# Attention and two feed-forward layers: weight conversions inside the attention steps, at other steps and on other engines

## The chip, the cores and the metric

The kernel runs on one core of one Trainium2 chip. The metric is the device time of one execution in microseconds (us), here the median of several runs. A profile is one execution, taken apart by engine: PE (TensorE), DVE (VectorE), ACT (ScalarE), POOL (GpSimd) and SP (SyncE, which here issues the transfers).

## The reference

Attention over 2 batches, 8 heads, 768 tokens and head size 64, with a bias that falls with distance and a mask (8 global keys and a window of 96), then two feed-forward layers of 512 to 2048 to 512, over 1536 tokens:

```
scores = q @ k^T / sqrt(D) - slope_h * dist        (masked where neither global nor local)
a = exp(scores - max)
a = a / (sum(a) + 1e-9)
x = a @ v
h = x @ w_in;   x = (h * tanh(softplus(h))) @ w_out
h = x @ w_in2;  x = bent(h) @ w_out2               (0 below -1, h above 1, a parabola between)
```

The weights arrive as 64-bit floats. The kernel turns each into a sum of two rounded 32-bit parts (hi and lo) on the chip, and each product of the layers is three matmuls: hi by hi, lo by hi and hi by lo.

## The kernel before

The attention runs in 24 steps, three for each of the 8 pairs of heads (2 batches by 4); a step is two blocks of 128 queries for the two heads of a pair. `attention_windows` writes the steps in a software pipeline, and the order that is written is the order on every engine (the schedule is manual). In step s stand, in this order: SyncE's loads; the rounding of finished outputs (`x_hi`, ScalarE); the scores of step s+1, the transposes of step s-2 and the value products of step s-3 (TensorE); the first half of the scores of step s (`softmax`: a reduction on VectorE that adds the bias, then the exponential on ScalarE, which also sums the totals); `normalise` of step s-1; the lower parts of the outputs (`x_lo`, VectorE); the eviction of one half of the transposes (ScalarE); the second half of the scores; the eviction of the other half (VectorE); and then what the table `BESIDE` (L36) names for step s.

`normalise` (L347) takes the totals of a step: it adds 1e-9 (VectorE, L349), forms the reciprocal (VectorE, L350) and scales the probabilities with it (four operations on GpSimd, L354). The transposes of that step read what is scaled. `st` is the small tile of the totals, `pr` the probabilities, `pts` the evicted transposes.

The table's entries are pieces of other work. `b2` to `b7` are the bias of one head (384 columns by a slope), on the engine that `BIAS_ON` names. The other names stand for one operation on one half (512 columns) of one of the first three weight blocks. The digit behind the letter is the block, the last one the half:

- T: `top` (L223), scales the upper words in place in the landing area (GpSimd, by `FIRST_ON`)
- B: `low` (L227), part of the lower words into `wbits` (ScalarE)
- V: `signed_value` (L246): the sign bits into `wbits` (VectorE, L233), and then shift and join (VectorE, L236)
- H: `high` (L240), the rounding of `wbits` to the hi part `whi` (ScalarE)
- R: `rest` (L243), what remains, to the lo part `wlo` (VectorE)

So T00 is the scaling of the first half of block 0. `wbits` holds one block at a time. A block is one transfer of 1 MB; blocks 0 and 1 land in the two `stage` buffers, block 2 in `third`. These loads stand in SyncE's queue between those of queries, keys and values (`wts.load` in L396; two more follow where V11 and V21 stand).

From step 23 on the entries h0a, h0b, h1a, h1b and g0a to g0c are the first pieces of the feed-forward layers, which then run on TensorE to the end. The functions that the diff touches, and what calls them:

Of the kernel before, what the change touches and what calls it, by code (L numbers as in the profile page):

```python
# [13 lines left out]
U16 = mybir.dt.uint16  # L14
I64 = mybir.dt.int64
AF = mybir.ActivationFunctionType
ALU = mybir.AluOpType
# [10 lines left out]
PRE = 3  # L28

BIAS_ON = "vvappppv"  # L30
FIRST_ON = "ppaavv"
LATER_ON = "aaaavv"

BESIDE = {  # L36
# [5 lines left out]
}  # L42


@with_exitstack
def attention_then_two_ffn_kernel(
# [10 lines left out]
    nc = tc.nc  # L57
    B, NP, _, S = q.shape
    H, D = 2 * NP, P // 2
# [49 lines left out]
    first = ctx.enter_context(tc.tile_pool(name="first", bufs=1))  # L109
# [31 lines left out]
    words = raw.bitcast(U32).rearrange("p (n two) -> p n two", two=2)  # L141
# [46 lines left out]
    class Weights:  # L188
# [15 lines left out]
        def convert(self, pool, m, f):  # L204


            hi, lo = (pool.tile([P, 2, DM], F32R, tag=f"w{n}{f}", name=f"w{n}{m}_{f}") for n in ("hi", "lo"))
            self.parts[m, f] = (hi, lo)
            first = m == 0 and f < PRE
            out = wbits  # L210

            def words(dtype, i, k):
                n = 8 // mybir.dt.size(dtype)
                return self.landing(m, f).bitcast(dtype).rearrange("p (a n w) -> p a n w", a=2, w=n)[:, i, :, k]

            bits = out.rearrange("p a (n two) -> p a n two", two=2)
            on = FIRST_ON if first else LATER_ON

            def moved(i, dtype):

                return words(dtype, i, 1) if first else wsc[:, i].bitcast(dtype)

            def top(i):  # L223

                scaled(on[i], moved(i, F32), words(F32, i, 1), 2.0 ** -112)

            def low(i):  # L227

                nc.scalar.activation(bits[:, i, :, 0], words(U16, i, 1), AF.Copy, scale=2.0 ** -13,  # L229
                                     bias=2.0 ** -14 - 0.5)  # L230

            def sign(i):
                nc.vector.tensor_scalar(bits[:, i, :, 1], words(U16, i, 3), 0x8000, None, op0=ALU.bitwise_and)  # L233

            def value(i):
                nc.vector.scalar_tensor_tensor(out[:, i].bitcast(U32), moved(i, U32), 3,  # L236
                                               out[:, i].bitcast(U32),
                                               op0=ALU.logical_shift_left, op1=ALU.bitwise_or)

            def high(i):  # L240
                rounded(on[2 + i], hi[:, i], out[:, i].bitcast(F32))

            def rest(i):  # L243
                remainder(on[4 + i], lo[:, i], out[:, i].bitcast(F32), hi[:, i])

            def signed_value(i):  # L246
                sign(i)
                value(i)

            def begin():  # L250

                if self.late:
                    self.late.pop(0)()
                top(0)
                low(0)
                sign(0)

            def middle():
                if self.late:
                    self.late.pop(0)()  # L260
                value(0)

            def end():
                top(1)
                low(1)
                sign(1)
                self.load()
                high(0)
                value(1)
                rest(0)  # L270
                self.late = [lambda: high(1), lambda: rest(1)]

            named = {f"{c}{f}{i}": lambda part=part, i=i: part(i) for i in range(2)
                     for c, part in (("T", top), ("B", low), ("V", signed_value), ("H", high), ("R", rest))}
            return named, (begin, middle, end)

        def finish(self):
# [8 lines left out]
    def attention_windows(x_hi, x_lo, bank, wts, opening):  # L286
        with ExitStack() as es:
# [58 lines left out]

            def normalise(s):  # L347
                pr, st = probs[s]
                nc.vector.tensor_scalar(st[..., 2], st[..., 1], 1e-9, None, op0=ALU.add)  # L349
                nc.vector.reciprocal(st[..., 3], st[..., 2])  # L350
                for u in range(2):
                    n = keys(2 * steps[s][2] + u)
                    for j in range(2):
                        nc.gpsimd.tensor_scalar(pr[:, u, j, 0:n], pr[:, u, j, 0:n], st[:, u, j, 3:4], 1.0,  # L354
                                                op0=ALU.mult, op1=ALU.mult)
# [37 lines left out]
                bias_of(h)  # L393
            for s in range(-1, NU + 4):

                if s in (0, 4, 10):  # L396
                    wts.load()
                if s >= 2 and s % 3 == 2 and s // 3 + 3 < len(pairs):
                    load_qk(rp, *pairs[s // 3 + 3])
                if s >= 6 and s % 3 == 0 and s // 3 + 1 < len(pairs):  # L400
                    vs[pairs[s // 3 + 1]] = load_v(rp, *pairs[s // 3 + 1])
                ready, done[:] = done[:], []
                for hi, lo, src in ready:
                    rounded("a", hi, src)
                if s + 1 < NU:
                    scores(s + 1)
                if 0 <= s - 2 < NU:
                    transposes(s - 2)
                if 0 <= s - 3 < NU:
                    values(s - 3)  # L410
                if 0 <= s < NU:
                    softmax(s, 0)
                if 0 <= s - 1 < NU:
                    normalise(s - 1)
                for hi, lo, src in ready:
                    remainder("v", lo, src, hi)
                if 0 <= s - 2 < NU:
                    evict(s - 2, 0)
                if 0 <= s < NU:
                    softmax(s, 1)  # L420
                if 0 <= s - 2 < NU:
                    evict(s - 2, 1)
                for name in BESIDE.get(s, ()):
                    opening[name]()
                    if name in ("V11", "V21"):
                        wts.load()


    def attention_all(x_hi, x_lo, bank, wts, opening):
        with ExitStack() as es:  # L430
# [31 lines left out]
            for b in range(B):  # L462
                for p in range(NP):
# [6 lines left out]
                    for j in range(2):  # L470
                        h = 2 * p + j
                        ro = slice(j * D, (j + 1) * D)
                        for pv, (t0, n) in zip(pvs, pieces):
                            for i in range(t0 // P, (t0 + n) // P):
# [3 lines left out]
                                for u, (k0, kn) in enumerate(((0, 4), (4, NB - 4))):  # L478
                                    for c in range(kn):
# [3 lines left out]
                                                            scale, None, op0=ALU.mult)  # L483
# [20 lines left out]
                                                     pT[:, c], start=(c == 0), stop=(c == NB - 1))  # L504
                    for pv, (t0, n) in zip(pvs, pieces):
                        split(x_hi[b][:, p, t0:t0 + n], x_lo[b][:, p, t0:t0 + n], pv)
            for name in sum((BESIDE[s] for s in sorted(BESIDE)), ()):
                if name[0] != "b":
                    opening[name]()
                    if name in ("V11", "V21"):  # L510
                        wts.load()
# [256 lines left out]
```

## Time and profile before

| | us |
|---|---|
| median of 3 runs | 626.03 (625.89 to 627.49) |
| span of the profiled execution, first to last instruction | 624.8 |
| PE busy in it | 603.2 |
| DVE busy | 419.2 |
| ACT busy | 390.8 |
| POOL busy | 53.2 |

The record gives the profiled execution no time other than its span; the median of the runs lies 1.2 us above that. Busy time counts instructions, not waits. Matmuls are pipelined, so TensorE's busy time is not a measure of how near to its peak it works. GpSimd works in the first 86 us alone, and all that the change touches lies there.

### The profile page before, as it was taken

Reading aid. Unit: us, or ns where it says so; the run is one execution under the profiler, and the core shown is the slowest. Engines: PE = TensorE matmul, PEld = TensorE weight load, DVE = VectorE, ACT = ScalarE, POOL = GpSimd, SP = SyncE. Lnnn points to the kernel's source line nnn. Section 1 sums busy time; section 2 is a strip of 40 time slices with the busy share of each in tenths; the row PEclk is TensorE's granted clock in tenths of the full one; section 3 lists DMA queues with packets and bytes.
Section 4 is the critical chain, followed back from the end, with each engine's and each line's share of the span. In section 5 each row is a group of like instructions: output and inputs, shape, how many; then the busy total and the mean of one; then the engine's idle time right before and its main releaser. Section 6 shows DMA issues by size and latency. Waiting matters only on the chain.

```text
span 624.8 us, 9737 instructions
## 1 busy us (share of the span) xinstructions
PE 603.2 (97%) x3584; PEld 510.7 (82%) x3584; DVE 419.2 (67%) x979; ACT 390.8 (63%) x848; POOL 53.2 (9%) x116
## 2 busy tenths in 40 slices
PE   5899899999999999999999999999999999999995
PEld 4677678888888888888888888888888888888884
DVE  6799969999999777797887876564333333433332
ACT  5899968888888566686776777574433333433332
POOL 3675630000000000000000000000000000000000
PEclk9988999999999999999999999999999999999999
DMA  7996302443333202121321422300100000100002
GB/s 201 310 287 229 116 1 69 135 135 121 102 122 131 68 1 68 68 83 59 129 69 67 135 69 73 129 1 1 67 1 1 1 1 0 68 0 2 0 1 72
DMA packets 10422, 49.85 MB, mean 80 GB/s; under 512 B 1408, under 2 KB 1664, under 8 KB 6272
## 3 DMA queue, kind: packets, MB, share of 16 engines
q1 hardware_dynamic: 10224, 48.90, 24.3%
q8 instruction: 30, 0.49, 0.3%
q10 hardware_dynamic: 144, 0.26, 0.1%
q14 instruction: 24, 0.20, 0.1%
HBM read 46.01 MB, written 3.15 MB: 79 GB/s over the span
## 4 chain that ended last, share of the span: by engine, by line
PE 88%; DVE 5%; ACT 3%; issue 1%; POOL 1%; DMA 1%; SPq 1%; POOLq 0%; DVEq 0%; ACTq 0%
PE psum L581 22%; PE psum L590 21%; PE psum L524 14%; PE psum L525 14%; PE psum L527 14%; ACT pr L344 2%; DVE pr L339 2%; PE psum L387 1%; PE psum L327 1%; POOL pr L354 1%; PE psum L368 1%; DVE pts L172 1%; DVE wbits L236 1%; DMA qr<-in_q_dram 1%; ACT pts L170 0%
## 5 line engine op out<-in xcount | busy, mean ns | idle before, releaser
L524 PE MATMUL psum<-x_hi,whi 128*128 128x512 f32 x448 | 157.1, 360 | 0.0
L525 PE MATMUL psum<-x_lo,whi 128*128 128x512 f32 x448 | 157.0, 360 | 0.0
L527 PE MATMUL psum<-x_hi,wlo 128*128 128x512 f32 x448 | 106.1, 359 | 0.0
L524 PEld LDWEIGHTS psum<-x_hi,whi 128*128 128x128 f32 x448 | 84.4, 188 | 14.8 <-issue 0.7
L525 PEld LDWEIGHTS psum<-x_lo,whi 128*128 128x128 f32 x448 | 84.5, 189 | 12.8
L527 PEld LDWEIGHTS psum<-x_hi,wlo 128*128 128x128 f32 x448 | 77.7, 189 | 12.5
L570 DVE TENSOR_TENSOR g_lo<-e,g_hi 128x512 fp32r<-128x512 f32 (+1 forms) x113 | 66.1, 608 | 31.6 <-ACT g_hi L568 31.5
L548 ACT ACTIVATE e<-psum 128x512 f32<-128x512 f32 (+1 forms) x49 | 28.8, 589 | 88.5 <-PE psum L527 88.5
L568 ACT ACTIVATE g_hi<-e 128x512 fp32r<-128x512 f32 (+1 forms) x113 | 59.8, 557 | 34.8 <-DVE e L553 31.2
L549 DVE TENSOR_SCALAR e<-e 128x512 f32<-128x512 f32 (+1 forms) x49 | 20.7, 422 | 83.8 <-ACT e L548 83.7
L590 PE MATMUL psum<-whi,g_hi 128*128 128x512 f32 x192 | 74.8, 390 | 0.0
L590 PE MATMUL psum<-whi,g_lo 128*128 128x512 f32 x192 | 74.7, 389 | 0.0
L590 PE MATMUL psum<-wlo,g_hi 128*128 128x512 f32 x192 | 74.7, 389 | 0.0
L581 PE MATMUL psum<-g_lo,whi 128*128 128x512 f32 (+1 forms) x256 | 67.2, 343 | 0.0
L581 PE MATMUL psum<-g_hi,wlo 128*128 128x512 f32 (+1 forms) x256 | 65.8, 338 | 0.0
L581 PE MATMUL psum<-g_hi,whi 128*128 128x512 f32 (+1 forms) x256 | 65.7, 338 | 0.0
L533 ACT ACTIVATE e<-psum 128x512 f32<-128x512 f32 x64 | 31.2, 492 | 51.3 <-PE psum L527 50.8
L553 DVE TENSOR_TENSOR e<-psum,e 128x512 f32<-128x512 f32 (+1 forms) x49 | 33.4, 681 | 30.7 <-ACT e L550 30.5
L344 ACT ACTIVATE pr<-pr,st 128x256 f32<-128x256 f32 (+1 forms) x96 | 46.0, 481 | 8.8 <-DVE st L339 7.7
L229 ACT ACTIVATE wbits<-stage 128x512 uint16<-128x512 uint16 x62 | 48.4, 781 | 1.3 <-DMA stage<-in_w_dram 1.3
L236 DVE SCALAR_TENSOR_TENSOR wbits<-wsc,wbits 128x512 uint32<-128x512 uint32 x58 | 40.2, 693 | 12.7 <-ACT wbits L229 9.5
L354 POOL TENSOR_SCALAR pr<-pr,st 128x256 f32<-128x256 f32 (+1 forms) x96 | 45.3, 492 | 28.0 <-ACT pr L344 12.6
(66 smaller groups left out, 896.2 us busy)
## 6 DMA issues: line engine op xcount, KB each, us to landing
stage<-in_w_dram SPq DMA_DIRECT2D x31, 1024.0 KB, 4.9
vr<-in_v_dram SPq DMA_DIRECT2D x8, 704.0 KB, 9.4
kr<-in_k_dram SPq DMA_DIRECT2D x14, 216.0 KB, 10.4
out_dram<-stage SPq DMA_DIRECT2D x11, 256.0 KB, 2.3
qr<-in_q_dram SPq DMA_DIRECT2D x7, 384.0 KB, 10.5
third<-in_w_dram SPq DMA_DIRECT2D x1, 1024.0 KB, 12.2
kr<-in_k_dram SPq DMA_DIRECT2D x2, 144.0 KB, 3.4
qr<-in_q_dram SPq DMA_DIRECT2D x1, 256.0 KB, 3.5
```

The source lines that it names most:

```text
L229: nc.scalar.activation(bits[:, i, :, 0], words(U16, i, 1), AF.Copy, scale=2.0 ** -13, bias=2.0 ** -14 - 0.5)
L236: nc.vector.scalar_tensor_tensor(out[:, i].bitcast(U32), moved(i, U32), 3, out[:, i].bitcast(U32), op0=ALU.logical_shift_left, op1=ALU.bit ...
L344: nc.scalar.activation(pr[:, u, j, 0:n], pr[:, u, j, 0:n], AF.Exp, scale=-1.0, bias=st[:, u, j, 0:1], accum_out=st[:, u, j, 1:2])
L354: nc.gpsimd.tensor_scalar(pr[:, u, j, 0:n], pr[:, u, j, 0:n], st[:, u, j, 3:4], 1.0, op0=ALU.mult, op1=ALU.mult)
L524: nc.tensor.matmul(ph, wh[:, c], xh[:, c, tok], start=(c == 0), stop=False)
L525: nc.tensor.matmul(ph, wh[:, c], xl[:, c, tok], start=False, stop=False)
L527: nc.tensor.matmul(ph, wl[:, c], xh[:, c, tok], start=False, stop=(c == KD - 1))
L553: nc.vector.tensor_tensor(e, ph, e, op=ALU.max)
L568: nc.scalar.activation(hi[:, t0:t0 + n], e, AF.Copy)
L570: nc.vector.tensor_tensor(lo[:, t0:t0 + n], e, hi[:, t0:t0 + n].bitcast(F32), op=ALU.subtract)
L581: nc.tensor.matmul(y, lhs[:, w], rhs[:, t0:t0 + n], start=(f == 0 and i == 0 and c % share == 0), stop=(f == NF - 1 and i == 2 and c % sha ...
L590: nc.tensor.matmul(ys[c], lhs[:, w], rhs, start=(f == 0 and i == 0), stop=(f == NF - 1 and i == 2))
```

## The change

The table of what stands beside the attention becomes two tables. `BESIDE` keeps what stands at the end of a step. `AHEAD` names one GpSimd operation a step, put inside `normalise`, behind the reciprocal in the code and ahead of the four scalings. V is split: S (the sign) becomes an entry of its own and V is shift and join alone. Of the first three blocks, T and now S run on GpSimd; H and R both run on VectorE (`FIRST_ON`). The addition of 1e-9 moves to GpSimd. The entries move: T00 from the end of step 5 to `normalise` in step 6, B00 from step 6 to 8, V00 from 7 to 9, H00 from 8 to 10, and so on; the last R moves from step 22 to 21. The second and third load of a block move from steps 4 and 10 to 3 and 7.

```diff
-FIRST_ON = "ppaavv"
+FIRST_ON = "ppvvvv"
...
 BESIDE = {
-    1: ("b2", "b3"), 3: ("b4",), 4: ("b5",), 5: ("T00",), 6: ("b6", "T01", "B00"), 7: ("b7", "V00", "B01"),
-    8: ("V01", "H00"), 9: ("H01", "R00"), 11: ("R01", "T10", "B10"), 12: ("T11", "V10", "B11"),
-    13: ("V11", "H10"), 14: ("R10", "H11"), 16: ("R11",), 17: ("T20", "B20"), 18: ("T21", "V20", "B21"),
-    19: ("V21", "H20"), 20: ("R20", "H21"), 22: ("R21",),
+    1: ("b2",), 6: ("b7",), 8: ("B00",), 9: ("V00",), 10: ("H00", "R00", "B01"), 11: ("V01",),
+    12: ("H01", "R01", "B10"), 13: ("V10",), 14: ("H10", "R10", "B11"), 15: ("V11",), 16: ("H11", "R11"),
+    17: ("B20",), 18: ("V20",), 19: ("H20", "R20", "B21"), 20: ("V21",), 21: ("H21", "R21"),
     23: ("h0a",), 24: ("h0b",), 25: ("g0a", "h1a", "g0b"), 26: ("g0c", "h1b"),
 }
+AHEAD = {
+    1: ("b3",), 2: ("b4",), 4: ("b5",), 5: ("b6",), 6: ("T00",), 7: ("S00",), 8: ("T01",), 9: ("S01",),
+    10: ("T10",), 11: ("S10",), 12: ("T11",), 13: ("S11",), 15: ("T20",), 16: ("S20",), 17: ("T21",), 18: ("S21",),
+}
...
             def sign(i):
-                nc.vector.tensor_scalar(bits[:, i, :, 1], words(U16, i, 3), 0x8000, None, op0=ALU.bitwise_and)
+                to, word = bits[:, i, :, 1], words(U16, i, 3)
+                if first:
+                    nc.gpsimd.tensor_scalar(to, word, 32768.0, 32768.0, op0=ALU.is_ge, op1=ALU.mult)
+                else:
+                    nc.vector.tensor_scalar(to, word, 0x8000, None, op0=ALU.bitwise_and)
...
             def normalise(s):
                 pr, st = probs[s]
-                nc.vector.tensor_scalar(st[..., 2], st[..., 1], 1e-9, None, op0=ALU.add)
+                nc.gpsimd.tensor_scalar(st[..., 2], st[..., 1], 1e-9, 1.0, op0=ALU.add, op1=ALU.mult)
                 nc.vector.reciprocal(st[..., 3], st[..., 2])
+                for name in AHEAD.get(s + 1, ()):
+                    opening[name]()
...
-                if s in (0, 4, 10):
+                if s in (0, 3, 7):
                     wts.load()
```

GpSimd's order from the scaling of step 4 to that of step 7, before. `pr4` is the probability tile of step 4, `stage0` the landing area of block 0 (the first such row is T00, the second T01), and `bias` here the entry b6:

```order
L354 TENSOR_SCALAR pr4_341<-pr4_341,st4_342 128x256 x4
L166 TENSOR_SCALAR stage0_77<-stage0_77 128x512
L354 TENSOR_SCALAR pr5_391<-pr5_391,st5_392 128x256 x4
L166 TENSOR_SCALAR bias_180<-wsc_80 128x384
L166 TENSOR_SCALAR stage0_77<-stage0_77 128x512
L354 TENSOR_SCALAR pr6_441<-pr6_441,st6_442 128x128 x2
L354 TENSOR_SCALAR pr6_441<-pr6_441,st6_442 128x256 x2
L354 TENSOR_SCALAR pr7_492<-pr7_492,st7_493 128x256 x4
```

The same stretch now (L352 is the addition to the totals, L169 with `stage0` T00 and then T01, L238 the sign S00):

```order
L169 TENSOR_SCALAR bias_180<-wsc_80 128x384
L359 TENSOR_SCALAR pr4_341<-pr4_341,st4_342 128x256 x4
L352 TENSOR_SCALAR st5_392<-st5_392 128x4
L169 TENSOR_SCALAR stage0_77<-stage0_77 128x512
L359 TENSOR_SCALAR pr5_391<-pr5_391,st5_392 128x256 x4
L352 TENSOR_SCALAR st6_442<-st6_442 128x4
L238 TENSOR_SCALAR wbits_79<-stage0_77 128x512
L359 TENSOR_SCALAR pr6_441<-pr6_441,st6_442 128x128 x2
L359 TENSOR_SCALAR pr6_441<-pr6_441,st6_442 128x256 x2
L352 TENSOR_SCALAR st7_493<-st7_493 128x4
L169 TENSOR_SCALAR stage0_77<-stage0_77 128x512
L359 TENSOR_SCALAR pr7_492<-pr7_492,st7_493 128x256 x4
```

T00 still stands between the scalings of step 4 and step 5; T01 stands one scaling later than before, b6 earlier, a sign has come in, and an addition stands ahead of each step's scalings.

VectorE's order through the end of step 12, before (L172 evicts the transposes of step 10; L233 is the sign and L236 the shift and join of V10, the first half of block 1):

```order
L172 COPY pts10_726<-psum_143 128x8x64
L233 TENSOR_SCALAR wbits_79<-stage1_78 128x512
L236 SCALAR_TENSOR_TENSOR wbits_79<-stage1_78,wbits_79 128x512
L339 ISA pr13_801,st13_802<-psum_143,bias_180 128x256
L339 ISA st13_802 128x1
L339 ISA pr13_801,st13_802<-psum_143,bias_180 128x256
L339 ISA st13_802 128x1
L349 TENSOR_SCALAR st12_750<-st12_750 128x4
L350 RECIPROCAL st12_750<-st12_750 128x4
```

And now (L175 CAST is the rounding H01, L178 the remainder R01, both of block 0; L353 is the reciprocal):

```order
L175 COPY pts10_724<-psum_143 128x8x64
L175 CAST whi0_0_146<-wbits_79 128x512
L178 TENSOR_TENSOR wlo0_0_147<-wbits_79,whi0_0_146 128x512
L342 ISA pr13_799,st13_800<-psum_143,bias_180 128x256
L342 ISA st13_800 128x1
L342 ISA pr13_799,st13_800<-psum_143,bias_180 128x256
L342 ISA st13_800 128x1
L353 RECIPROCAL st12_748<-st12_748 128x4
```

The addition has left VectorE, and a rounding and a remainder of block 0 stand where the sign and the value of block 1 stood.

## Rows read from the trace of the kernel before

**Rows 1.** Busy us (instructions) by stretch: PE, PEld, DVE, ACT, POOL; clock; DMA; GB/s

```profile
35.50:60.00 24.50, 22.47 (x298) 19.32 (x298) 23.90 (x101) 23.09 (x79) 15.64 (x32) 0.93 0.86 257
60.00:82.50 22.50, 19.20 (x261) 15.84 (x257) 22.04 (x86) 21.38 (x73) 14.88 (x31) 1.00 0.30 106
82.50:95.00 12.50, 12.50 (x121) 10.13 (x120) 7.52 (x20) 6.90 (x18) 3.13 (x7) 1.00 0.00 1
```

**Rows 2.** Waits of the attention: who waited for whom, us, times, longest

```profile
DVE st L349 <- ACT pr L344: 0.9, 2, 0.6
```

**Rows 3.** GpSimd in order of time: start, us, operation, [idle before, what ended it]

```profile
26.60 0.65 POOL L166 TENSOR_SCALAR stage<-stage 128x512 f32<-128x512 f32 x1 [4.14 <-DMA stage<-in_w_dram]
27.22 1.85 POOL L354 TENSOR_SCALAR pr<-pr,st 128x256 f32<-128x256 f32 x4
```

**Rows 4.** Block 0: its issue in time; then its size and us to landing

```profile
11.58 0.52 SPq L202 DMA_DIRECT2D stage<-in_w_dram  x1
...
stage<-in_w_dram SPq DMA_DIRECT2D x1, 1024.0 KB, 14.9
```

**Rows 5.** TensorE in order of time, first and last of six groups without a pause

```profile
27.76 1.84 PE L368 MATMUL psum<-ident,pr 64*128 64x64 f32 x16 [2.44 <-POOL pr L354]
...
35.48 1.14 PE L327 MATMUL psum<-kr,qr 64*128 64x256 f32 x8
```

**Rows 6.** VectorE's groups to 84 us: busy, mean ns; last row ns least/median/most

```profile
L349 DVE TENSOR_SCALAR st<-st 128x4 f32<-128x4 f32 x24 | 4.8, 201 | 1.3 <-ACT pr L344 0.9
L175 DVE TENSOR_TENSOR wlo<-wbits,whi 128x512 fp32r<-128x512 f32 x6 | 4.6, 773 | 0.0
...
L175 DVE TENSOR_TENSOR wlo<-wbits,whi x6: 679/725/908, 38.1 to 80.0; 128x512 fp32r<-128x512 f32 x6
```

**Rows 7.** VectorE in order of time: the sign-and-value pairs of steps 12 and 19

```profile
47.14 0.74 DVE L233 TENSOR_SCALAR wbits<-stage 128x512 uint16<-128x512 uint16 x1
...
48.85 0.41 DVE L339 CUSTOM_DVE_ANT_0 pr<-psum,bias 128x256 f32<-128x256 f32 x1
...
70.67 0.51 DVE L233 TENSOR_SCALAR wbits<-third 128x512 uint16<-128x512 uint16 x1
71.29 0.74 DVE L236 SCALAR_TENSOR_TENSOR wbits<-third,wbits 128x512 uint32<-128x512 uint32 x1
71.95 0.41 DVE L339 CUSTOM_DVE_ANT_0 pr<-psum,bias 128x256 f32<-128x256 f32 x1
```

**Rows 8.** VectorE in order of time: a clamp with one input and its successor

```profile
90.41 0.43 DVE L535 TENSOR_SCALAR e<-e 128x512 f32<-128x512 f32 x1 [0.44 <-ACT e L533]
90.87 0.69 DVE L536 SCALAR_TENSOR_TENSOR e<-e 128x512 f32<-128x512 f32 x1
```

**Rows 9.** Two remainders on VectorE and the scaling on GpSimd at the same time

```profile
54.97 0.48 POOL L354 TENSOR_SCALAR pr<-pr,st 128x256 f32<-128x256 f32 x1
...
55.08 0.91 DVE L175 TENSOR_TENSOR wlo<-wbits,whi 128x512 fp32r<-128x512 f32 x1
...
60.47 0.73 DVE L175 TENSOR_TENSOR wlo<-wbits,whi 128x512 fp32r<-128x512 f32 x1
...
60.63 0.91 POOL L354 TENSOR_SCALAR pr<-pr,st 128x256 f32<-128x256 f32 x1
```

**Rows 10.** GpSimd: T in blocks 0 and 1 (ns least/median/most); one scaling of 128x128

```profile
L166 POOL TENSOR_SCALAR stage<-stage x4: 651/770/1120, 26.6 to 47.5; 128x512 f32<-128x512 f32 x4
...
59.48 0.38 POOL L354 TENSOR_SCALAR pr<-pr,st 128x128 f32<-128x128 f32 x1 [0.73 <-PE psum L368]
```

**Rows 11.** TensorE in order of time: the first hidden block's first matmul

```profile
82.47 0.50 PE L524 MATMUL psum<-x_hi,whi 128*128 128x512 f32 x1
```

**Rows 12.** The last query load of pair 5: issue, us to landing, first scores

```profile
29.19 0.33 SPq L96 DMA_DIRECT2D qr<-in_q_dram  x1
...
qr<-in_q_dram SPq DMA_DIRECT2D x1, 384.0 KB, 13.2
...
50.28 1.05 PE L327 MATMUL psum<-kr,qr 64*128 64x128 f32 x7 [0.96 <-DVE st L339]
```

More of the change, by code (lines that the diff above doesn't have):

```diff
@@ L244, in rest @@
                 remainder(on[4 + i], lo[:, i], out[:, i].bitcast(F32), hi[:, i])
-            def signed_value(i):
-                sign(i)
-                value(i)
             def begin():
@@ L273, in convert @@
             named = {f"{c}{f}{i}": lambda part=part, i=i: part(i) for i in range(2)
-                     for c, part in (("T", top), ("B", low), ("V", signed_value), ("H", high), ("R", rest))}
+                     for c, part in (("T", top), ("S", sign), ("B", low), ("V", value), ("H", high), ("R", rest))}
             return named, (begin, middle, end)
@@ L506, in attention_all @@
                         split(x_hi[b][:, p, t0:t0 + n], x_lo[b][:, p, t0:t0 + n], pv)
-            for name in sum((BESIDE[s] for s in sorted(BESIDE)), ()):
+            for name in sum((AHEAD.get(s, ()) + BESIDE.get(s, ()) for s in range(28)), ()):
                 if name[0] != "b":
```

## The prediction

> **What bounds the kernel now.** I read four views, in this order. First the busy time by stretch [rows 1]. From 82.5 us on TensorE is busy in all of the next 12.5 us, and no later work depends on the attention steps, so whatever moves the start of that stretch moves the end of the kernel one to one. Before it, in the attention steps, VectorE is the fullest engine: 23.90 of 24.5 us, then 22.04 of 22.5 us, with ScalarE close behind at 23.09 and 21.38 and GpSimd at about two thirds. The change is therefore priced as VectorE time inside the attention steps, up to the moment when TensorE starts the first hidden block at 82.47 us [rows 11].
>
> Second, the waits [rows 2]: VectorE seldom has to wait for the exponentials' totals. Third, GpSimd's order in time [rows 3]: it sits idle for 4.14 us before T00, the first scaling of a weight block, and the scaling of step 5 stands behind T00. T00 cannot begin before its megabyte has landed: issued at 11.58 us, 14.9 us to landing, so 26.5 us [rows 4]. Fourth, TensorE behind it: the transposes for step 5 start at 27.76, one scaling after T00, and six groups of matmuls follow each other without a pause until the scores at 35.48 us, of which the first and the last are shown [rows 5].
>
> **What cannot change: everything up to 35.5 us.** The words "begun later" suggest that this wait goes. It does not. In the changed order T00 still stands between the total of step 5 and the scaling of step 5, so the scaling still follows T00 and T00 still follows the landing at 26.5 us. Nothing ahead of this load in SyncE's queue is moved. The load of the second block stands in the same place of the queue as before (its step number changes, the order does not); only the third block's load goes ahead of the keys and queries of pair 5 and the values of pair 4, which then land some 4.1 us later (1 MB at the 257 GB/s of that stretch [rows 1]). The last query piece of pair 5 was issued at 29.19 us and landed 13.2 us later, at 42.4; its first scores start at 50.28 [rows 12]. So it lands at 46.5 us, in time; without this cover of 7.9 us the 4.1 would stand on the path.
>
> So gains of the first six steps (GpSimd's extra total, bias work one per step, VectorE's freed time) end in the same wait, and TensorE's gapless chain to 35.48 starts at the same moment. What differs at 35.5 us is what has been done: the old order has V00 and V01 behind it there, the new one has both still ahead, because B00 and B01 stand at steps 8 and 10.
>
> **VectorE from step 9 to the end of attention, before.** The totals: 15 additions of 201 ns [rows 6] = 3.0 us. Sign and value pairs: four (steps 12, 13, 18, 19), from the sign's start to the next step's first instruction 1.71 us in the first and 1.28 in the last [rows 7], 5.9 us in all four. Remainders: six at 773 ns [rows 6], of which 0.08 us overlap with the next instruction (the value at 71.29 ends at 72.03, the next starts at 71.95 [rows 7]), so 0.70 each = 4.2 us. Together 13.1 us.
>
> **The same, after.** Six values, six roundings, six remainders. A remainder that meets nothing is 0.68 us, the least of the six [rows 6], 0.60 with its overlap; a value, with two inputs of the same size, I put at 0.61. A rounding (a copy of 128x512 from SBUF to SBUF on VectorE) is not in the trace. The nearest row below is the clamp at 90.41, one input and the same size, 0.43 us and 0.46 to a next instruction that needs its result [rows 8]; the nearest above is a remainder, 0.60. I take 0.46, as it has one input like the clamp. The Trainium skill ("VectorE: DVE Perf Modes", the perf-mode tier table) gives fp32 copies and one-input operations in SBUF twice the rate of a two-input operation; the clamp against the least remainder agrees, 0.43 to 0.68. Sum without collisions: 6 x (0.61 + 0.46 + 0.60) = 10.0 us, 3.1 us less than before.
>
> **Collisions take part of it back.** VectorE and GpSimd hold each other up when VectorE works on two SBUF inputs. At 55.08 a remainder takes 0.91 us, while a scaling runs until 55.45; at 60.47 one takes 0.73, and the scaling that starts within it 0.91 instead of 0.48 [rows 9]. Against 0.68 VectorE loses 0.05 to 0.23 us, 0.14 in the middle, and GpSimd about 0.43. Now 12 groups (six values; six rounding-and-remainder pairs) stand just where GpSimd is scaling: 12 x 0.14 = 1.7 us. Bounds: none, and 0.23 for each of 18 instructions, 4.1 us.
>
> **The hop of the totals.** VectorE's reciprocal now waits for an addition on GpSimd, which stands behind the scaling of the step before, and behind the reciprocal wait the x remainder, the second half of the scores and the eviction on VectorE. An addition on 128x4 is not in the trace; a scaling of 128x256 takes 0.48 us [rows 9] and one of 128x128 0.38 [rows 10], so extrapolated to no elements 0.28 us, and with the passing on some 0.35 (an estimate). It costs only where VectorE is there before the total is: before the change it had to wait for the exponentials in 2 of 24 steps, 0.9 us [rows 2]. I take 0.4 us; bounds 0 and 1.8 (a third of 15 x 0.35).
>
> **GpSimd** then does in a step an addition 0.28, a T or sign operation of about 0.65, and four scalings 1.85 [rows 3, 10]: 2.8 us, plus about 0.4 lost to VectorE, against steps of 3.1 us (15 steps from 35.48 to 82.47 [rows 5, 11]). It has next to no room left, but is not the bound. ScalarE loses six roundings, some 3 us, and is not the bound from step 9 to 21.
>
> **Sum:** 10.0 + 1.7 + 0.4 = 12.1 against 13.1 us: TensorE's dense part starts 1.0 us earlier. On the profiled execution, span 624.8 to 623.8 us. The median of the runs, 626.03, is 1.2 above the span, so 625.0 us. The measurement of this kernel tells about 0.3% (1.9 us) from no change.
>
> **The rivals.**
> *Forecast: VectorE stays the bound, collisions eat two thirds of the saving.* 625.0 us, with a range of its own of 624.2 to 627.5.
> *Faster: the collisions do not grow.* For: GpSimd's scalings wait for the reciprocal and have pauses, and the old pairs collided too (1.71 against 1.28 us [rows 7]). Against: GpSimd's pauses get filled. Then the gain is 3.1 us, and up to 3.8 if the rounding overlaps its successor (0.34): 622.2 to 622.9; with half of it 624.
> *Slower: the sign on GpSimd is dear and GpSimd becomes the bound.* A compare-and-multiply on strided 16-bit words is not in the trace; the nearest row is T, 0.65 us at the least and 0.77 in the middle [rows 10], and I take 0.65. From about 0.95 us on (3.1 less 0.28 and 1.85; GpSimd's lost time falls on its scalings, which have more slack) the next addition comes late, VectorE's reciprocal waits for it, and everything behind waits too. At 2.0 us, three T operations, each of six signs costs about 1.0 us: 626.0 - 1.0 + 6 = 631 us. The Trainium skill ("GPSIMD Engine Reference", elementwise, side-by-side cycle accounting) puts data-dependent branching at about 12 cycles an element; worked out from its figures as an estimate, a sign done that way is 5.1 us for 512 elements, well past that point; no row here has a comparison of this kind.
> *Slower: rounding at full price and a visible hop.* 0.14 more for six roundings, the hop at 1.8, collisions at 3 us: 10.8 + 1.8 + 3 = 15.6 against 13.1, so 628.5 us.
> *The change does not do what it says:* the wait at 26.5 us stays; that is in the forecast. Were it gone, 4.1 us of GpSimd's wait would go too: 621 us.
>
> **How the numbers follow.** Forecast within 0.3% 0.50. Collisions that do not grow 0.31, and the wait gone 0.03: faster 0.34. Dear signs 0.09, dear rounding and hop 0.07: slower 0.16. The range reaches from 622.2 (the faster rival's end) to 628.5 (the second slower one); the rest of 2 in 10 is dear signs and a vanished wait.
>
> **What would show it.** In the changed profile T00 on GpSimd still begins at about 26.6 us after a wait of some 4 us for the load, and TensorE's row at 35.48 stands within 0.2 us. The six roundings on VectorE take 0.43 to 0.7 us; values and remainders on average more than 0.69 and 0.77. GpSimd's additions take about 0.25 and its sign operations 0.6 to 0.8 us. TensorE's first hidden block starts near 81.5 us. It is wrong if the sign takes over 1 us, if VectorE waits for GpSimd's addition by more than 1.8 us in all after step 9, if VectorE is no longer the fullest engine from 35.5 to 60 us, or if the wait at 26.5 us is gone.

## The result, and the profile after

The changed kernel takes 631.96 us (median of four runs, 631.33 to 633.31), the kernel before 625.96 beside it: a ratio of 1.0096, with a 95% interval of 1.0081 to 1.0112. It is slower by 6.0 us, outside the forecast range of 622.2 to 628.5. The profiled execution took 631.62 us, with a span of 629.8 (before: 624.8).

The busy time by stretch comes first, with the columns of [rows 1].

```profile
35.50:60.00 24.50, 21.77 (x236) 16.44 (x233) 19.64 (x77) 19.43 (x64) 22.91 (x38) 0.89 0.77 215
60.00:82.50 22.50, 20.75 (x251) 16.31 (x249) 19.30 (x78) 19.07 (x66) 19.50 (x37) 0.90 0.37 136
82.50:95.00 12.50, 11.20 (x140) 9.27 (x140) 7.59 (x28) 7.32 (x26) 7.36 (x17) 1.00 0.01 2
```

GpSimd (fifth busy number) was at 15.64 of 24.5 us and is now at 22.91. VectorE (third) fell from 23.90 to 19.64. GpSimd has become the engine with the least room. The attention also reaches past 82.5 us: GpSimd is busy for 7.36 us there, before for 3.13.

The waits of the attention answer to [rows 2]: who waited for whom, us in total, times, longest.

```profile
DVE st L353 <- POOL st L352: 16.0, 16, 2.2
PEld psum L373 <- POOL pr L359: 13.6, 30, 1.5
ACT pts L173 <- PE psum L373: 10.6, 11, 2.5
```

Before, VectorE waited for the totals for 0.9 us; now it waits 16.0 us for GpSimd's additions (L352), 8.4 of them from 35.5 to 88 us. TensorE's transposes wait for GpSimd's scalings (L359), and ScalarE's evictions for the transposes. Before, these two were shorter:

```profile
PEld psum L368 <- POOL pr L354: 5.7, 10, 2.8
ACT pts L170 <- PE psum L368: 6.8, 5, 2.5
```

GpSimd in order of time shows what holds it (start, us, operation, idle time before it), first from the addition ahead of T00 on, and then through steps 11 and 12 into step 13. L238 is the sign, L169 on `stage` a T.

```profile
23.95 0.20 POOL L352 TENSOR_SCALAR st<-st 128x4 f32<-128x4 f32 x1
26.28 0.65 POOL L169 TENSOR_SCALAR stage<-stage 128x512 f32<-128x512 f32 x1 [2.13 <-DVE bias L167]
26.91 1.86 POOL L359 TENSOR_SCALAR pr<-pr,st 128x256 f32<-128x256 f32 x4
28.85 0.20 POOL L352 TENSOR_SCALAR st<-st 128x4 f32<-128x4 f32 x1
29.13 2.15 POOL L238 TENSOR_SCALAR wbits<-stage 128x512 uint16<-128x512 uint16 x1
...
43.82 0.20 POOL L352 TENSOR_SCALAR st<-st 128x4 f32<-128x4 f32 x1
44.10 2.14 POOL L238 TENSOR_SCALAR wbits<-stage 128x512 uint16<-128x512 uint16 x1
46.20 2.08 POOL L359 TENSOR_SCALAR pr<-pr,st 128x256 f32<-128x256 f32 x4
48.36 0.20 POOL L352 TENSOR_SCALAR st<-st 128x4 f32<-128x4 f32 x1
48.65 0.70 POOL L169 TENSOR_SCALAR stage<-stage 128x512 f32<-128x512 f32 x1
49.29 2.05 POOL L359 TENSOR_SCALAR pr<-pr,st 128x256 f32<-128x256 f32 x4
51.43 0.52 POOL L352 TENSOR_SCALAR st<-st 128x4 f32<-128x4 f32 x1
```

GpSimd has no wait from 43.82 to 51.43: each operation starts within 0.1 us of the end of the one before. A step with a sign takes GpSimd 4.54 us (addition to addition, 43.82 to 48.36), a step with a T 3.07 us (48.36 to 51.43). The sign takes 2.14 us where the prediction had put 0.65. All six are dear in the view of line L238 (ns least/median/most, first and last start):

```profile
L238 POOL TENSOR_SCALAR wbits<-stage x4: 2129/2138/2152, 29.1 to 52.0; 128x512 uint16<-128x512 uint16 x4
L238 POOL TENSOR_SCALAR wbits<-third x2: 2131/2237/2343, 63.0 to 70.2; 128x512 uint16<-128x512 uint16 x2
```

VectorE in order of time, in steps 10 and 12, is the other side of it:

```profile
42.06 0.44 DVE L175 CAST whi<-wbits 128x512 fp32r<-128x512 f32 x1
42.53 0.85 DVE L178 TENSOR_TENSOR wlo<-wbits,whi 128x512 fp32r<-128x512 f32 x1
...
48.60 0.18 DVE L353 RECIPROCAL st<-st 128x4 f32<-128x4 f32 x1 [1.62 <-POOL st L352]
```

The rounding costs 0.44 us, about as forecast; the 1.62 us before the reciprocal are the wait for the addition of 48.36, which stands behind the sign and the scalings. TensorE's first hidden block ([rows 11], 82.47 before) starts 5.6 us later, which is the loss to within half a microsecond:

```profile
88.07 0.50 PE L529 MATMUL psum<-x_hi,whi 128*128 128x512 f32 x1
```

### The profile page after: what moved, and what is told of

It reads as the page before. It is cut to its first block, busy times and chain, and to the rows that moved or that the text cites. A ratio compares the mean times of both kernels' runs of the same rounds, so it can differ in the third digit from the quotient of the medians.

```text
span 629.8 us, 9776 instructions
## 1 busy us (share of the span) xinstructions
PE 609.3 (97%) x3584; PEld 512.7 (81%) x3584; DVE 414.3 (66%) x955; ACT 389.0 (62%) x842; POOL 72.0 (11%) x146
## 4 chain that ended last, share of the span: by engine, by line
PE 87%; DMA 6%; POOL 3%; DVE 2%; issue 1%; SPq 0%; ACT 0%; ACTq 0%; DVEq 0%
PE psum L586 22%; PE psum L595 21%; PE psum L529 14%; PE psum L530 14%; PE psum L532 14%; DMA stage<-in_w_dram 2%; POOL pr L359 2%; DMA kr<-in_k_dram 1%; PE psum L392 1%; DMA qr<-in_q_dram 1%; PE psum L373 1%; PE psum L330 1%; DVE pr L342 1%; DMA counts_raw<-in_counts_dram 0%; DVE pts L175 0%
## 5 line engine op out<-in xcount | busy, mean ns | idle before, releaser
L359 POOL TENSOR_SCALAR pr<-pr,st 128x256 f32<-128x256 f32 (+1 forms) x96 | 45.8, 499 | 4.5 <-DVE st L353 2.3
## 6 DMA issues: line engine op xcount, KB each, us to landing
third<-in_w_dram SPq DMA_DIRECT2D x1, 1024.0 KB, 14.5
```

## The experiments

Two theories stand against each other at first. A: the sign on GpSimd is dear and everything behind it waits. B: the totals' hop to GpSimd is dear whatever the sign costs. A third, C, blames the roundings on VectorE. Later runs ask what is left of the change without the sign. A ratio is always to the kernel before on the same chip, with its 95% interval; it need not equal the quotient of two medians.

**e1: the signs back on VectorE**, in front of shift and join, the rest as changed.

```diff
-    1: ("b3",), 2: ("b4",), 4: ("b5",), 5: ("b6",), 6: ("T00",), 7: ("S00",), 8: ("T01",), 9: ("S01",),
+    1: ("b3",), 2: ("b4",), 4: ("b5",), 5: ("b6",), 6: ("T00",), 8: ("T01",),
...
-                if first:
-                    nc.gpsimd.tensor_scalar(to, word, 32768.0, 32768.0, op0=ALU.is_ge, op1=ALU.mult)
-                else:
-                    nc.vector.tensor_scalar(to, word, 0x8000, None, op0=ALU.bitwise_and)
+                nc.vector.tensor_scalar(to, word, 0x8000, None, op0=ALU.bitwise_and)
...
```

> The changed kernel with one part undone: the sign is again taken on VectorE, right ahead of shift and join, and GpSimd's list has no signs. Theory A (the sign on GpSimd costs 2.13 us instead of the 0.65 assumed, six of them hold up the scalings and the additions behind them): GpSimd's load in a sign step falls from 0.28 + 2.13 + 1.85 = 4.3 us to 2.1, VectorE gets six signs of about 0.6 us back (3.6 us), so of the 6.0 us lost some 5 to 6.5 come back: 625.5 to 627. Theory B (the reciprocal's wait for an addition on another engine is what costs, 16 us in all in the changed kernel): the hop is still there, no less than 629.5. Theory C (roundings on VectorE and their collisions): no less than 630.

Measured: 626.59 us, ratio 1.0015 (0.9994 to 1.0036), the first hidden block at 84.28 us. The loss of 6.0 us goes, as near as the interval tells, when the signs leave GpSimd, with the totals still there; B had asked for no less than 629.5 us, C for no less than 630. The row of 35.5 to 60 us and VectorE's wait:

```profile
35.50:60.00 24.50, 21.19 (x286) 17.72 (x284) 23.50 (x86) 21.02 (x72) 18.44 (x39) 1.00 0.95 248
...
DVE st L354 <- POOL st L353: 8.3, 11, 2.6
```

VectorE is the fullest again (23.50), GpSimd at 18.44, and the wait for the additions is half of the 16.0 us.

**e2: the totals back on VectorE**, the signs on GpSimd.

```diff
-                nc.gpsimd.tensor_scalar(st[..., 2], st[..., 1], 1e-9, 1.0, op0=ALU.add, op1=ALU.mult)
+                nc.vector.tensor_scalar(st[..., 2], st[..., 1], 1e-9, None, op0=ALU.add)
```

> The changed kernel with one part undone: the 1e-9 is added on VectorE again. Theory A: the scalings still stand behind signs of 2.13 us; a step with a sign saves at most the addition's 0.28 us on GpSimd, the others some 0.2: 629.5 to 631.5. Theory B: VectorE no longer waits for GpSimd, and of the 6.0 us nearly all come back: 626 to 627.5. Theory C: no less than 630.5.

Measured: 631.24 us, ratio 1.0079 (1.0051 to 1.0108), hidden block at 86.95. Almost the whole loss stays when the hop is gone: B falls.

**e3: the roundings back on ScalarE**, the signs and totals on GpSimd (`FIRST_ON = "ppaavv"`).

> The changed kernel with one part undone: the six roundings are on ScalarE again. Theory A: VectorE has waits to spare in these steps, so that the time stays, 631 to 632.5. Theory B: the same. Theory C: six roundings of 0.44 to 0.71 us and the remainders' collisions go, 3 to 5 us come back: 627 to 629.

Measured: 634.91 us, ratio 1.0131 (1.0088 to 1.0174). C falls; A had expected no difference, and missed too. The new tables put H and R of one half into the same step, so that VectorE's remainder stands right behind the other engine's rounding:

```profile
DVE wlo L178 <- ACT whi L173: 5.9, 6, 1.5
```

**m1: the sign's price by itself.** The kernel before with 18 GpSimd operations behind the attention, three each of six forms, every one 512 columns wide: compare-and-multiply and multiply-and-multiply, on 16-bit words spread as the sign's are, on 16-bit words side by side, and on 32-bit floats.

```diff
...
+            for to, frm, op0, op1 in (
+                (d2, s4, ALU.is_ge, ALU.mult),
+                (d2, s4, ALU.mult, ALU.mult),
+                (d16[:, 0:512], s16[:, 0:512], ALU.is_ge, ALU.mult),
+                (d16[:, 0:512], s16[:, 0:512], ALU.mult, ALU.mult),
+                (d32[:, 0:512], f2, ALU.is_ge, ALU.mult),
+                (d32[:, 0:512], f2, ALU.mult, ALU.mult),
+            ):
...
```

> The kernel before, with 18 additional operations on GpSimd behind the attention steps, three of each form over 512 columns: the sign as in the change (16-bit words, one in four read, one in two written, compare and multiply), the same with two multiplications, both on words that lie side by side, and 32-bit floats (one in two read) with compare and multiply and with two multiplications. Only their durations matter; the time of the kernel is not compared. If the compare is what is dear, the compare rows take about 2.1 us in each type and the multiplications about 0.65; if the 16-bit type is, both its rows take about 2.1 and the float rows 0.65; if it is the stride, the rows with words side by side fall to about 0.65.

The rows are GpSimd in order of time, the first from the start of all 18 operations, each later one from the start of the next form on (start, us to the end of the last, operations left):

```profile
84.98 27.17 POOL L442 TENSOR_SCALAR bias<-third 128x512 uint16<-128x512 uint16 x18
91.70 20.44 POOL L442 TENSOR_SCALAR bias<-third 128x512 uint16<-128x512 uint16 x15
94.65 17.50 POOL L442 TENSOR_SCALAR bias<-third 128x512 uint16<-128x512 uint16 x12
101.11 11.03 POOL L442 TENSOR_SCALAR bias<-third 128x512 uint16<-128x512 uint16 x9
103.91 8.23 POOL L442 TENSOR_SCALAR bias<-third 128x512 f32<-128x512 f32 x6
110.06 2.08 POOL L442 TENSOR_SCALAR bias<-third 128x512 f32<-128x512 f32 x3
```

A third of the difference of two starts is one operation. Comparisons: (91.70 - 84.98) / 3 = 2.24 us spread, (101.11 - 94.65) / 3 = 2.15 side by side, (110.06 - 103.91) / 3 = 2.05 in floats. Multiplications: 0.98, 0.93 and 0.69 us (2.08 / 3). Neither the type nor the spacing (tried in 16-bit words) makes the sign dear; the comparison does.

**e5: the sign as a multiplication.** The changed kernel with a multiplication in place of the comparison, everything in its place. It leaves the signs of the first three blocks out.

```diff
-                    nc.gpsimd.tensor_scalar(to, word, 32768.0, 32768.0, op0=ALU.is_ge, op1=ALU.mult)
+                    nc.gpsimd.tensor_scalar(to, word, 0.0, 1.0, op0=ALU.mult, op1=ALU.mult)
```

> The changed kernel with the sign on GpSimd as a multiplication by 0 in place of the compare, on the same 16-bit words: the first three weight blocks lose their signs, so this kernel leaves the sign out of its result; all else is the changed kernel. In the forms measured on GpSimd the compare took 2.0 to 2.4 us and the multiplication on the same words 0.87. Theory A (the compare's price alone made the change slower): each sign is some 1.3 us shorter, the time falls to 624.5 to 627. Rival D (six more operations on GpSimd in these steps cost the time by holding up VectorE, whatever each takes): no less than 629.5.

Measured: 624.94 us, ratio 0.9986 (0.9974 to 0.9999), the hidden block at 80.46. The line of the sign, the stretch and the wait for the additions (20 to 82.5 us):

```profile
L238 POOL TENSOR_SCALAR wbits<-stage x4: 765/778/789, 28.9 to 47.9; 128x512 uint16<-128x512 uint16 x4
...
35.50:60.00 24.50, 21.87 (x290) 18.19 (x286) 24.27 (x92) 22.24 (x78) 21.66 (x45) 1.00 0.83 237
...
DVE st L353 <- POOL st L352: 6.4, 7, 3.0
```

With the sign at 0.78 us the time is the 625.0 of the forecast, though not in the way that it forecast (next section). The comparison is all that e5 takes out of the change, so it makes the 7.0 us from here to 631.96: six signs are longer by 2.17 - 0.78 = 1.39 us each, 8.3 in all, and 84% of that reaches the end.

**e6: the wait for block 0 taken away in the kernel before.** Most pieces of blocks 0 and 1 come one or two steps later; T00 stands at the end of step 7.

```diff
-    1: ("b2", "b3"), 3: ("b4",), 4: ("b5",), 5: ("T00",), 6: ("b6", "T01", "B00"), 7: ("b7", "V00", "B01"),
-    8: ("V01", "H00"), 9: ("H01", "R00"), 11: ("R01", "T10", "B10"), 12: ("T11", "V10", "B11"),
-    13: ("V11", "H10"), 14: ("R10", "H11"), 16: ("R11",), 17: ("T20", "B20"), 18: ("T21", "V20", "B21"),
+    1: ("b2", "b3"), 3: ("b4",), 4: ("b5",), 6: ("b6",), 7: ("b7", "B00", "T00"), 8: ("V00", "T01", "B01"),
+    9: ("V01", "H00"), 10: ("H01", "R00"), 12: ("R01", "T10", "B10"), 13: ("T11", "V10", "B11"),
+    14: ("V11", "H10"), 15: ("R10", "H11"), 16: ("R11",), 17: ("T20", "B20"), 18: ("T21", "V20", "B21"),
```

> The kernel before, with the pieces of the first two weight blocks one to three steps later (T00 at the end of step 7 instead of 5), engines as before. By the reading of the wait before T00 (4.1 us, and everything behind it up to 35.5 us), GpSimd no longer waits for the load, and 3 to 4 us go: 621.5 to 623. If the load's wait only hides another bound (the transfers of keys and queries behind it, or VectorE's work, which is then pressed into fewer steps), under 1.5 us go: 624 to 625.5.

Measured: 623.91 us, ratio 0.9969 (0.9954 to 0.9983); the hidden block at 80.63. GpSimd in order of time, to be held against [rows 3]:

```profile
27.29 1.72 POOL L354 TENSOR_SCALAR pr<-pr,st 128x128 f32<-128x128 f32 x4 [0.43 <-DVE st L350]
28.99 0.67 POOL L166 TENSOR_SCALAR stage<-stage 128x512 f32<-128x512 f32 x1
```

T00 waits for nothing, and the scalings of two steps more are done ahead of it. By the medians 1.8 us go (625.72 beside it), between the two expectations and under half of the 4.14 us. Other pieces moved too, so this is not the price of the wait alone.

**e8: signs and totals on VectorE**, the rest as changed (the edits of e1 and e2 together).

> The changed kernel with two parts undone, signs and additions of 1e-9 both on VectorE; against e1_sign_dve it tells what the addition on GpSimd costs or saves by itself. By the prediction's sum VectorE gets 3.0 us of additions back and loses 0.4 us of waiting, so this is 2 to 3 us slower than e1_sign_dve: 628.5 to 629.5. If the hop costs what the profile of e1_sign_dve shows (VectorE waits 8.3 us for GpSimd's additions), it is 1 to 3 us faster than it: 623.5 to 625.5.

Measured: 633.08 us, ratio 1.0118 (1.0101 to 1.0135). Against e1 the totals on GpSimd give 6.5 us by the medians, though one addition each for 24 steps is 4.8 us [rows 6]; both expectations are missed. The profiled executions differ by less, hidden block at 87.43 against 84.28; that of e1 (628.30 us) lay above its median and that of e8 (631.50) below. The direction is settled by these runs, the size is not.

**e9: signs on VectorE, roundings on ScalarE**, totals on GpSimd (e1 and e3 together).

> The changed kernel with two parts undone, the signs on VectorE and the roundings on ScalarE; against e1_sign_dve it tells what the roundings on VectorE cost or save without the dear compare. By the prediction's sum they cost VectorE some 2.8 us and their collisions, so without them 623 to 625. If what e3_round_act showed holds here too (the remainder on VectorE then waits for ScalarE's rounding in the same step), it is 2 to 4 us slower than e1_sign_dve: 628.5 to 630.5.

Measured: 633.62 us, ratio 1.0131 (1.0115 to 1.0148), 7 us slower than e1, where the nearer expectation was 2 to 4. VectorE's remainders wait for the roundings as in e3:

```profile
DVE wlo L178 <- ACT whi L173: 7.7, 6, 1.5
```

In these tables, where a remainder stands in the same step as its rounding, the rounding belongs on VectorE.

**c1: a version from what was learnt.** Totals on GpSimd, one GpSimd operation ahead of the scalings, signs on VectorE, roundings on ScalarE but a step ahead of the remainder, T00 in `normalise` in step 8; the loads of blocks stand where the change has them. Against the kernel before:

```diff
...
+    1: ("b2",), 6: ("b7",), 7: ("B00",), 8: ("V00", "B01"),
+    9: ("V01", "H00"), 10: ("H01", "R00"), 12: ("R01", "B10"), 13: ("V10", "B11"),
+    14: ("V11", "H10"), 15: ("R10", "H11"), 16: ("R11",), 17: ("B20",), 18: ("V20", "B21"),
...
+AHEAD = {
+    1: ("b3",), 2: ("b4",), 4: ("b5",), 5: ("b6",), 8: ("T00",), 9: ("T01",),
+    13: ("T10",), 14: ("T11",), 18: ("T20",), 19: ("T21",),
+}
...
-                nc.vector.tensor_scalar(st[..., 2], st[..., 1], 1e-9, None, op0=ALU.add)
+                nc.gpsimd.tensor_scalar(st[..., 2], st[..., 1], 1e-9, 1.0, op0=ALU.add, op1=ALU.mult)
```

> Edit: the signs are on VectorE and the roundings on ScalarE, as in the kernel before; of the change only the totals' 1e-9 is on GpSimd; the pieces of blocks 0 and 1 come one to three steps later as in e6, so that T00 stands at the end of step 8. Theory that VectorE bounds the stretch: e6's 623.9 us less a part of the some 24 additions that VectorE no longer runs at 0.2 us and less again for the hop, 621 to 623 us, with VectorE waiting less than 3 us for the additions. Rival, that the hop to GpSimd costs VectorE what the addition gave: VectorE waits 6 to 8 us for the additions as in e1 and e5 and the time is 624 to 627 us. The first hidden block tells it: before 80.6 us or after it.

Measured: 622.44 us, ratio 0.9951 (0.9934 to 0.9968): 3.7 us faster than the kernel before by the medians (626.16 beside it), the best of all. The stretch, the wait for the additions (0 to 95 us), a reciprocal with its wait, and the first hidden block:

```profile
35.50:60.00 24.50, 21.35 (x284) 17.50 (x282) 23.39 (x94) 23.51 (x81) 19.76 (x42) 1.00 0.90 250
...
DVE st L355 <- POOL st L354: 4.9, 10, 0.9
...
42.49 0.18 DVE L355 RECIPROCAL st<-st 128x4 f32<-128x4 f32 x1 [0.44 <-POOL st L354]
...
78.16 0.50 PE L531 MATMUL psum<-x_hi,whi 128*128 128x512 f32 x1
```

VectorE and ScalarE are equally full, and GpSimd has room for the additions. The longest wait for one is 0.9 us; in all they are 4.9 us where under 3 was expected.

**c2: e1 with T00 in `normalise` in step 8** and T01 in step 9, so that T00 does not wait for its load.

> Edit: e1 (the change with the signs on VectorE) with T00 moved to the end of step 8 and T01 to step 9. Theory that the 2 to 3 us that GpSimd still stands before T00 is on the path: e1's 626.6 us less about 2, 624 to 625 us, and T00 waits for nothing. Rival, that VectorE alone bounds the stretch and GpSimd's wait is covered: 626 to 627 us.

Measured: 625.74 us, ratio 0.9989 (0.9969 to 1.0009), between the two expectations. The interval overlaps that of e1 (0.9994 to 1.0036): not settled. The remaining 2.6 us of e1's wait are worth 1.6 us (0.0026 of 626) at a guess from the ratios, and perhaps nothing.

**c3 and c4: c1 with the totals on VectorE, and c1 again**, on one chip. The edit of c3 is that of e2; c4 is c1 unchanged.

> Edit: c1_later_total_pool (622.4 us) with the 1e-9 back on VectorE; nothing else differs. Theory that the addition on GpSimd earns its place once GpSimd has room and VectorE is nearly full (23.39 of 24.5 us in c1): 24 additions of 0.2 us come back to VectorE, of which the some 14 behind step 9 lie on the path, 2.8 us less what c1's waits for them cost; 623.5 to 625.5 us, first hidden block after 79.2 us. Rival, that the hop costs what the addition gives and c1's gain over e6 (623.9) is the one operation a step ahead of the scalings: within 0.5 us of c1, 622 to 623 us.

> The same kernel as c1_later_total_pool, run again beside c3_later_total_dve so that the two are compared on one chip. Expected within 0.15% of 622.4 us if c1's time is its own, 623.5 to 625 us if c1's seven runs were a lucky draw.

Measured: c3 624.41 us, ratio 0.9978 (0.9965 to 0.9991); c4 622.36 us, ratio 0.9955 (0.9941 to 0.9969). The stretch in c3:

```profile
35.50:60.00 24.50, 21.08 (x290) 17.56 (x284) 23.84 (x95) 23.49 (x80) 16.33 (x31) 1.00 0.96 279
```

c1's time repeats, and the totals on GpSimd are worth 2.05 us in this order, by medians (the intervals just overlap). c3 and e6 (623.91) differ in the T operations' place ahead of the scalings and one step later, and in the places of biases and loads; all that is worth nothing that these runs can tell.

## Why the prediction was wrong, point by point

**The sign's price: wrong, and it makes the loss.** The mis-sized term is the 0.65 us for a sign on GpSimd; it is 2.13 to 2.34 us. The prediction took the nearest row by engine and size, the scaling T [rows 10]. That row is a multiplication, and the operation differs in just the respect that counts: m1 has comparisons at 2.05 to 2.24 us and multiplications at 0.69 to 0.98 in every type. The end at the other side, 2.0 us, stood in the text and gave 631, but its chance was put at 0.09 and the range stopped at 628.5. No row excluded it, so it belonged inside the range.

The Trainium skill ("GPSIMD Engine Reference", elementwise, side-by-side cycle accounting) was cited there for a dear comparison, 5.1 us by its figure as an estimate. The measurement, 2.14 us, decides: the estimate is more than twice too high for this operation, but it pointed the right way, and the row did not. Whether this comparison is branching of that kind, no run shows.

**The rival's mechanism: right in kind and size.** It said that from 0.95 us on the next addition comes late and the reciprocal waits. With the measured mean of 2.17 us its working gives 625.0 + 6 x (2.17 - 0.95) = 632.3 us; 631.96 came. Against e5 the same working gives 7.3 us, and 7.0 came. VectorE's waits for the additions rose to 16.0 us (8.4 from step 9 to the first hidden block, where the prediction had named 1.8 as a sign of being wrong), GpSimd became the fullest, and VectorE's freed time turned into waiting.

**GpSimd's step of 2.8 us, "not the bound": the step that failed.** With the sign at 2.14 us and not 0.65 a step with a sign is 4.54 us instead, against the 3.1 of a step before, and GpSimd becomes the bound. The half of that step without the sign held: the addition is 0.20 us (0.28 forecast) and a step with a T 3.07 us, against 2.8 and 0.4 lost to VectorE.

**VectorE's sum: the prices about right, the gain not seen.** Roundings were 0.51 us on average (six, 417 to 712 ns) against a price of 0.46, values 0.72, remainders 0.79. Above their undisturbed durations that is (0.51 - 0.43) + (0.72 - 0.69) + (0.79 - 0.68) = 0.22 us for a group, 1.3 us for six; 1.7 was forecast for the collisions. But e5, where the sign is cheap, does not show the 1.0 us that the sum had promised behind 35.5 us. In the profiled executions, one of each kernel, its scores of that time are done 1.9 us earlier than before (34.68 against 36.62 us, next paragraph but one), and its first hidden block starts 2.0 us earlier (80.46 against 82.47). So 1.9 us came where the forecast had none, and 0.1 where it had 1.0. That e5's 624.94 us agrees with the forecast is luck, as far as these executions show: a gain ahead of 35.5 us stands in for one that was forecast behind it.

**The hop: too low.** From step 9 to the first hidden block VectorE waits 1.9 us for additions in e5, where 0.4 was put and 1.8 was the bound. The rest of the 6.4 us lies in earlier steps, among it the wait of 3.0, which stands behind T00 and its load. From 33.5 to 82.5 us:

```profile
DVE st L353 <- POOL st L352: 1.9, 3, 0.7
```

This wait is what the sum lacked: with it, and with e5's collisions (1.4 us, worked out as above from 0.45, 0.77 and 0.82 us), the prediction's terms give 10.0 + 1.4 + 1.9 = 13.3 us against 13.1, no gain, as measured. The price of having the totals on VectorE instead came out at 2.05 us (c3 against c4) and 6.5 us (e8 against e1); the prediction's 3.0 less 0.4 lies between.

**Everything up to 35.5 us: half right.** T00 starts at 26.28 us, as forecast within 0.3 us. The idle time before it is 2.13 us and not 4, because the scaling of step 4 came later, hardly because the block came sooner. Its row names b7 (`bias`, VectorE), which ends at 26.23 us; T00 does not read that, and block 0, issued at 11.73 us and 14.5 us to landing, is there at the same moment. The scores that stood at 35.48 us are in a row that starts at 34.35, earlier, and in TensorE's order of time they are done at 35.83 against 36.62:

```profile
34.35 1.26 PE L330 MATMUL psum<-kr,qr 64*128 64x256 f32 x7
35.32 0.34 PE L373 MATMUL psum<-ident,pr 64*128 64x64 f32 x3
35.45 0.38 PE L330 MATMUL psum<-kr,qr 64*128 64x256 f32 x1
```

So the chain behind T00 was not as fixed as the text said, and it could not be: the granted clock in 20 to 35.5 us was 1.00 here and 0.78 before. The prediction had read six groups without a pause as a fixed length. By the scaling of step 8 the lead is lost (38.23 against 36.75 us): two signs already stand ahead of it. e5, with short signs, keeps its lead: the same scores end at 33.55 + 1.13 = 34.68 us, T00 starts at 26.03, and the granted clock from 26 to 35.5 us was 0.82 against 0.64 before. Why the clock came back earlier is not shown.

```profile
33.55 1.13 PE L330 MATMUL psum<-kr,qr 64*128 64x256 f32 x8
```

**The faster rivals: over-priced.** For a vanished wait the prediction had put 4.1 us; e6 takes the wait away in the kernel before and gains 1.8. Collisions that do not grow were to give 3.1 us; that leaves out the hop, by the prediction's own 0.4 a gain of 2.7, and the collisions did grow, by the 1.3 us above.

## What to carry to other kernels

Price an operation that moves to another engine by a row with the same arithmetic, not the same size; where none exists, time that one operation by itself, or keep the whole gap in the range. An engine that serves every step (here GpSimd, whose scalings and additions all others wait for) sets the pace as soon as its step is longer than that of the others (here 4.54 us, where a step had taken 3.1); ask for its longest step, not its mean busy share. In these tables a producer and its consumer on two engines needed a step between them (c1); in the same step they did better on one engine (e1 against e9).

## What the runs showed of the hardware

A comparison (`is_ge`) followed by a multiplication in one instruction on GpSimd costs 2.0 to 2.3 us for 512 columns, two to three times two multiplications (0.7 to 1.0 us). It is dear in 16-bit words and in floats, and in 16-bit words with or without gaps (m1). An operation on 128x4 costs 0.20 us there.

TensorE's clock fell again in the changed kernel: 0.89 and 0.90 in the two stretches where it paused for GpSimd's scalings, 1.00 in the same stretches of e5. Two rows of TensorE in order of time show sixteen value products at either level, the first after a pause of 0.42 us before the transposes ahead of it:

```profile
40.70 1.97 PE L392 MATMUL psum<-pts,vr 128*64 128x128 f32 x16
...
44.56 1.09 PE L392 MATMUL psum<-pts,vr 128*64 128x128 f32 x16
```

The granted clock is 0.51 in the stretch of the first and 1.00 in that of the second: at 2.4 GHz they take 1.09 us, close to 1.2 GHz 1.97.

How much of the loss is this, and how much GpSimd's queue itself, is in part on record. From T00 on (26.28 us) to 56.3 us GpSimd has no wait in the changed kernel, so there its queue alone sets the pace. T00 starts 0.25 us later than in e5, and at the end of that stretch the reciprocal of the same step comes 5.3 us later (changed kernel, then e5):

```profile
56.35 0.18 DVE L353 RECIPROCAL st<-st 128x4 f32<-128x4 f32 x1 [1.14 <-POOL st L352]
...
51.08 0.18 DVE L353 RECIPROCAL st<-st 128x4 f32<-128x4 f32 x1
```

So of the 7.6 us between the two first hidden blocks (88.07 and 80.46) 5.0 are the queue's. For the remaining 2.6 it was not separated.
